# Last weight tap in two transfers, scratch loads a round sooner, and the last tile's inverse jobs a little later in a one-core FFT convolution

## The chip, the core and the metric

The kernel runs on one core of a Trainium2 chip. A core has a matrix engine (TensorE, PE in the profile, its weight loads PEld), a vector engine (DVE), a scalar engine (ACT), GpSimd (POOL) and SyncE (SP), which here issues nearly all DMA transfers, one after the other. ACT issues a few in the last tile. The metric is the time of one execution in microseconds on the device. Three executions of the kernel before took 270.08, 270.45 and 270.87 us; the median is 270.45 us.

## What is computed

The input `x` has 224 x 224 pixels of 96 channels, the weights `w` 7 x 7 taps of 96 x 96. The reference multiplies their two-dimensional transforms, which makes a circular convolution over the picture:

```python
wp = jnp.pad(w, ((0, H - K), (0, W - K), (0, 0), (0, 0)))
Xf = rfft2(x, axes=(1, 2))
Wf = rfft2(wp, axes=(0, 1))
Yf = jnp.einsum('bhwi,hwio->bhwo', Xf, Wf)
y  = irfft2(Yf, s=(H, W), axes=(1, 2)).astype(jnp.bfloat16)
```

## The kernel before

**Stages.** Along the height the kernel works with short transforms: 28 output rows need 34 input rows, and these become 17 slots (`NS`), most of them one complex frequency each. Along the width it convolves directly with the seven taps, split into even and odd pixels. Four stages follow from that.

- Weight preparation (`prep_jobs`). The raw weights lie in the tile `wq`, two rows for each of the 49 taps (a tap's input channels 0 to 47 and 48 to 95). A matmul of `wq` with a small matrix gives the transformed weights `WF` of a group of slots. Each of these matmuls reads columns from the whole length of `wq`, so the first of them needs every column of all 98 rows.
- Stage A (`a_jobs`, `f_jobs`): a matmul of 118 pixel rows with `Fm` gives the transformed pixels `xf`.
- Stage B (`b_round`): for one slot, DVE forms differences and sums `J` of `xf`; PE multiplies `xf` and `J` with `WF` (33 matmuls a round); ACT and DVE combine the sums in PSUM (tiles `tt_`, `u`, `v`), and POOL or DVE writes `yf`. Every three slots `yf` goes to a scratch tensor in DRAM (`scr`).
- Stage C (`c_jobs`): a tile's scratch comes back in another layout (`tt`, `tt2`), so that slots lie on partitions; a job is two matmuls with `Gm`, two evacuations, and now and then a store to `out`.

**Tiles.** The picture is cut into seven tiles of 32 columns. Tiles 0 and 1 run interleaved, tiles 2 to 6 one after the other, 17 rounds each. A round has two half rounds, and in the middle and at the end of a round `fills` lets other jobs in: `add(a, b, jobs)` spreads a list of jobs evenly over the half rounds from a to b. Stage A of the next tile and stage C of an earlier one are such lists. `CQ[t]` says how many jobs of tile t-2 and how many of tile t-1 run in tile t: in tile 5 four old and eleven new ones, in tile 6 (the last, `TL`) eleven new ones. The order of the instructions on every engine is the order of the program; there is no scheduler behind it.

**The scratch loads.** `queue_c(t - 1)` puts the five loads of tile t-1 (four `tt` and one `tt2`, the latter in four transfers) on a list, and `pump` issues from it as long as fewer than four `tt` buffers and one `tt2` buffer are taken. A finished unit of jobs frees its buffer and pumps again. In the kernel before, `queue_c` is called at round 3 of the tiles 2 to 6. SP waits in order, so a load that waits for the last scratch store of the tile before holds up what stands behind it.

**The start.** SP issues in this order: the halo pixels of both pixel groups (four transfers), the first tile's pixels of group 0 (two), ten weight transfers, then the pixels of group 1. The weights are cut into five chunks of columns; for each chunk the last tap's two rows go first and the 96 rows of the other taps second. The pixels of group 1 wait for the third chunk (`HOLD`). Every transfer counts on one of eight semaphores in turn, and waits for the transfer eight places before it. While the weights are under way PE runs dummy matmuls (`warm`): 17 at the start, and two times 11 between the first pixels' transforms and the weight preparation.

**The end.** In the last tile the scratch is in three parts. The first (slots 0 to 8, `scra`) is loaded back at round 11, the others (`scrb`) after the last round; then come 36 dummy matmuls, the second half of the inverse, and the last stores.

Of the kernel before, what the change touches and what calls it, by code (L numbers as in the profile page):

```python
# [17 lines left out]
NS = L // 2  # L18
# [29 lines left out]
HOLD = 2  # L48
# [8 lines left out]
def kernel(  # L57
# [7 lines left out]
    _, H, W, C = x.shape  # L65
    assert tuple(w.shape) == (KT, KT, C, C) and C == 96 and H == NJ * B and W % (2 * TW) == 0
    NT = W // (2 * TW)
    TL = NT - 1
    HB = JG * B
    R = HB + PAD  # L70
    PW = KT * KT
    FR = 2 * NS
    PW2 = 2 * PW
    C2 = C // 2
    assert NJ == 8
    SYNC = mybir.DependencyInfo(mybir.DependencyClass.Sync, mybir.DependencyReason.DATA)
# [57 lines left out]
    def dma(out_ap, in_ap):  # L134
        return DE.dma_start(out=out_ap, in_=in_ap)
# [18 lines left out]
    wqx = wtmp.tile([128, C - 1 + 127 * C + 1], BF16, name="wq")  # L154
    wq = wqx[0:PW2]
    WC = C * C - C2
# [18 lines left out]
    def load_x(t, jg):  # L175
        return load_rows(xbuf(t, jg), jg, t * 2 * TW, 2 * TW)

    wsrc = w.rearrange("kh kw i o -> (kh kw) (i o)")
# [2 lines left out]
    load_x(0, 0)  # L181
    wcut = [WC * c // NWC // 128 * 128 for c in range(NWC)] + [WC]
    wdma = []
    for c0, c1 in zip(wcut, wcut[1:]):
        for k, n in ((PW - 1, 1), (0, PW - 1)):
            wdma.append(dma(wqx[2 * k:2 * (k + n), c0:c1],
                bass.AP(wsrc.tensor, wsrc.offset + k * C * C + c0, [[C * C, n], [C2, 2], [1, c1 - c0]])))
    for d in load_x(0, 1):
        tc.add_manual_dep(d.ins, wdma[2 * HOLD + 1].ins.name, SYNC, reason="second pixels behind the weights")

    wu = cpool.tile([128, 128], BF16, name="wu")
    wur = wu[:].unsqueeze(1).to_broadcast([128, 4, 128])
# [2 lines left out]
    def warm(n):  # L195
        pwu = bank()
        for _ in range(n):
            TE.matmul(pwu[:].rearrange("p (a b) -> p a b", a=4), lhsT=wu[:, 0:128], rhs=wur, start=True, stop=True)
# [235 lines left out]
    def a_jobs(t):  # L434
        xf = new_xf(t)
        jobs = []
        for jg in range(2):
            for h in range(2):
                for (q, n) in ((0, 3), (3, 3), (6, 2)):
                    jobs.extend(a_bank(t, xf, xn_bufs[jg], h * PXC + 2 * q, n, jg, HALO + h * 8 + q))  # L440
            jobs.append(then_load(jobs.pop(), t + 1, jg))
        return jobs
# [23 lines left out]
    def jit(t, g):  # L466
        s0, s1 = JGB[g]
        n = s1 - s0
        xf = xf_tiles[t][0:C]
        xv = xf.rearrange("c p r s w j -> c p r s (w j)")  # L470
        b = jcount[0] % 3 if t < 2 else (jcount[0] - 2 * len(JGB)) % 2
        jcount[0] += 1
        Jb = J_bufs[b][0:C].rearrange("c (k s q) -> c k s q", k=7, s=3)
        for s in range(s0, s1):
            jbuf[(t, s)] = Jb[:, :, s - s0]

        def sub(o, a, b, op, cost):
            def f():
                load["v"] += 170 + cost / 1.92
                return VE.tensor_tensor(out=o, in0=a, in1=b, op=op)  # L480
            return f
        x0, x1 = xv[:, 0, :, s0:s1], xv[:, 1, :, s0:s1]
        c0, c1 = max(s0, REAL[0] + 1), min(s1, REAL[1])
        i0, i1 = c0 - s0, c1 - s0
        pd, rd, sd, qd = x1.ap
        dpl = bass.AP(x1.tensor, x1.offset - NJ, [pd, [NJ, 2], rd, sd, qd])
        return [
            sub(Jb[:, 0:4, 0:n].rearrange("c (k r) s q -> c k r s q", r=2), dpl,
                x0.unsqueeze(1).to_broadcast([C, 2, 2, n, PP]), ALU.subtract, 4 * PP * n),
            sub(Jb[:, 4, i0:i1], xv[:, 0, 0, c0:c1], xv[:, 0, 1, c0:c1], ALU.add, PP * (c1 - c0)),  # L490
            sub(Jb[:, 5:7, i0:i1], Jb[:, 0:4:2, i0:i1], Jb[:, 1:4:2, i0:i1], ALU.add, 2 * PP * (c1 - c0)),
        ]
# [152 lines left out]
    def c_jobs(t):  # L645
        jobs = []
        w0 = t * 2 * TW
        for gi, h in LT:
            hold = {}
            nq = 2 if gi < 2 else 3  # L650

            def mk_(q, gi=gi, h=h, nq=nq, hold=hold):
                def put(j0, nj, px, npx, row, col):
                    dma(out[0, j0 * B:(j0 + nj) * B, w0 + px:w0 + px + npx, :].rearrange("h w c -> h (w c)"),
                        hold["yo"][row:row + nj * B, col:col + npx * C])

                def f():
                    if q % 2 == 0:
                        hold["yo"] = new_yo()
                    tt = tt_tiles[(t, gi, h)]  # L660
                    yo = hold["yo"]
                    nj = 2 if q == 2 else 3
                    for b in range(2):
                        pb = bank()[0:nj * B, 0:4 * C]
                        TE.matmul(pb, lhsT=G[0:nj * FR, 0:nj * B],
                                  rhs=tt[0:nj * FR, 4 * q + 2 * b:4 * q + 2 * b + 2, :].rearrange("p w e -> p (w e)"), start=True, stop=True)
                        k = 2 * (q % 2) + b
                        evac(yo[0:nj * B, k * 4 * C:(k + 1) * 4 * C], pb, 4 * C)
                    if q == 1 and gi < 2:
                        put(gi * 3, 3, h * PXC, PXC, 0, 0)  # L670
                    elif q == 1:
                        put(6, 2, 0, 16, 0, 0)
                        for j in range(2):
                            put(6 + j, 1, 24, 8, 2 * B, j * 8 * C)
                    elif q == 2:
                        put(6, 2, 16, 8, 0, 0)
                    if q == nq - 1:
                        held[gi == 2] -= 1
                        pump()
                return f  # L680
            for q in range(nq):
                jobs.append(mk_(q))
        return jobs
# [11 lines left out]
    def queue_c(t):  # L695
        pend.extend((t, *k) for k in LT)
        pump()
# [6 lines left out]
    for p in range(3):  # L704
        for f in fj[p][0]:
            f()
    for n in (11, 11):
        warm(n)
    for f in prep_jobs(0):
        f()  # L710
# [22 lines left out]
    def fills(qs, k):  # L733
        def f():
            for q in qs:
                pace(q, k)
        return f
# [3 lines left out]
    def add(a, b, jobs):  # L741
        qs.append([a, b, jobs, len(jobs)])
# [15 lines left out]
    for r in range(NS + LAG):  # L758
# [32 lines left out]
        for t in range(2):  # L791
            s = r - LAG * t
# [15 lines left out]
    for t in range(2, NT):  # L808
        if t == TL:
            scr_tiles[t] = None  # L810
            scr_tiles[(t, 0)] = dr_pool.tile([TW, NJ, SA, 4 * C], BF16, name="scra")
            for i in range(2):
                scr_tiles[(t, 1 + i)] = dr_pool.tile([TW, NJ, (SB - SA, NS - SB)[i], 4 * C], BF16, name=f"scrb{i}")
        else:
            scr_tiles[t] = dr_pool.tile([TW, NJ, NS, 4 * C], BF16, name="scr")
        qs = []
        if t + 1 < NT:
            add(4 if t == 2 else 0, 26, a_jobs(t + 1))
        nold, nnew = CQ[t]
        k1 = 2 * NS if t < TL else 2 * NS - 9  # L820
        k0 = 10 if t in (2, TL) else 3
        km = k0 + -(-(k1 - k0) * nold // (nold + nnew))
        add(k0, km, cj[:nold])
        cn = c_jobs(t - 1)
        cj = cn[nnew:]
        add(km, k1, cn[:nnew])
        plan = {}
        for g, (s0, s1) in enumerate(JGB):
            if g + 1 < len(JGB) or t + 1 < NT:
                plan[s0 if g + 1 < len(JGB) else s0 - 1] = g  # L830
        for s in range(NS):
            now = ()
            if s in plan:
                g = plan[s]
                now = jit(t, g + 1) if g + 1 < len(JGB) else jit(t + 1, 0)
            if s == 3:
                queue_c(t - 1)
            if t in (3, 4):
                next(gp, None)
            if t == TL and s == SA + 2:  # L840
                sv = scr_tiles[(TL, 0)].rearrange("w j s (r e) -> (j s r) w e", r=2)
                for g in range(2):
                    for p0, p1 in ((0, 64), (64, KA)):
                        dma(tl_a[g][p0:p1], sv[g * KA + p0:g * KA + p1])
            b_round(t, s, fills(qs, 2 * s), fills(qs, 2 * s + 1), bool(now) or (t == TL and s >= NS - 3), now)
# [24 lines left out]
    for i, (g, q) in enumerate(order):  # L870
# [3 lines left out]
        k = i + 8 - LF  # L874
        if 8 <= k < len(order):
            live[order[k]] = first(*order[k])
        if q % 2 == 1:
            w0, c0 = TL * 2 * TW + (q - 1) * 4, (q % 4 - 1) * 4 * C
# [33 lines left out]
```

## Time and profile before

| | |
|---|---|
| profiled execution | 270.74 us, span on the core 269.0 us |
| granted TensorE clock, mean | 0.997 |
| PE busy | 257.9 us (96%), 5144 matmuls |
| DVE, ACT, POOL busy | 214.3, 195.5, 99.4 us |
| DMA | 46.78 MB, mean 174 GB/s |
| first matmul on the weights | 16.21 us |
| tile 5 begins, tile 6 begins | about 191 us, about 224 us |
| last matmul of stage B | 252.46 us |

All times inside the execution count from the start of its span. A busy PE in this table is not PE at its peak: matmuls are pipelined, and their ends are modelled. What decides is where PE waits. Idle time is listed with what ended it, for PE and for its weight loads (PEld) apart; the weight load stands ahead of its matmul and shows the longer idle time of the two. The helper that records every operation puts all of them on line 89, so groups are told apart by their tiles and not by lines.

### The profile page before, as it was taken

Reading aid. Unit: us, or ns where it says so; the run is one execution under the profiler, and the core shown is the slowest. Engines: PE = TensorE matmul, PEld = TensorE weight load, DVE = VectorE, ACT = ScalarE, POOL = GpSimd, SP = SyncE. Lnnn points to the kernel's source line nnn. Section 1 sums busy time; section 2 is a strip of 40 time slices with the busy share of each in tenths; the row PEclk is TensorE's granted clock in tenths of the full one; section 3 lists DMA queues with packets and bytes.
Section 4 is the critical chain, followed back from the end, with each engine's and each line's share of the span. In section 5 each row is a group of like instructions: output and inputs, shape, how many; then the busy total and the mean of one; then the engine's idle time right before and its main releaser. Section 6 shows DMA issues by size and latency. Waiting matters only on the chain.

```text
span 269.0 us, 12171 instructions
## 1 busy us (share of the span) xinstructions
PE 257.9 (96%) x5144; PEld 237.1 (88%) x5144; DVE 214.3 (80%) x457; ACT 195.5 (73%) x483; POOL 99.4 (37%) x156
## 2 busy tenths in 40 slices
PE   8899999999999999999999999999998999899993
PEld 3679999999998999999999998989997989779862
DVE  5649998889899788778787888777887889778724
ACT  5549988587974578988988789886986864467113
POOL 7782315363647435322322222234132242522100
PEclk9999999999999999999999999999999999999998
DMA  6948011811111597987976486989658834888866
GB/s 171 230 129 217 6 46 46 243 47 67 46 46 50 163 276 135 294 249 206 289 207 198 133 246 192 250 223 332 224 151 152 255 98 154 198 231 212 223 118 205
DMA packets 47014, 46.78 MB, mean 174 GB/s; under 512 B 35286, under 2 KB 37986, under 8 KB 46960
## 3 DMA queue, kind: packets, MB, share of 16 engines
q1 hardware_dynamic: 44672, 43.94, 59.2%
q10 hardware_dynamic: 2288, 2.06, 2.8%
q8 instruction: 40, 0.66, 1.1%
q14 instruction: 14, 0.11, 0.1%
HBM read 24.65 MB, written 21.33 MB: 171 GB/s over the span
## 4 chain that ended last, share of the span: by engine, by line
PE 64%; DMA 12%; DVE 11%; ACT 7%; issue 3%; SPq 2%; DVEq 0%; ACTq 0%
PE pb L89 64%; DMA tt<-scr 5%; DMA wq<-in_w_dram 5%; DVE J L89 4%; ACT WF L89 3%; ACT xf L89 2%; DVE v L89 2%; DVE WF L89 2%; SPq L89 2%; DMA xf<-scrb 2%; DVE u L89 1%; DMA scrb<-yf 1%; DVE yf L89 1%; DVE xf L89 0%; DVE tt L89 0%
## 5 line engine op out<-in xcount | busy, mean ns | idle before, releaser
L89 PE MATMUL pb<-WF,J 96*128 96x96 bf16 x2821 | 162.6, 206 | 1.1 <-DVE J L89 0.9
L89 PEld LDWEIGHTS <-J 96*128 96x128 bf16 x2821 | 138.0, 98 | 10.5 <-issue 2.2
L89 POOL TENSOR_TENSOR yf<-v,u 128x384 bf16<-128x384 f32 x79 | 81.4, 1042 | 147.3 <-issue 86.9
L89 ACT CAST xf<-pb 96x408 bf16<-96x408 f32 (+3 forms) x145 | 67.8, 490 | 8.9 <-PE pb L89 5.3
L89 PE MATMUL pb<-WF,xf 96*128 96x96 bf16 x952 | 59.9, 206 | 0.5 <-ACT xf L89 0.5
L89 DVE TENSOR_TENSOR J<-xf 96x1824 bf16<-96x1824 bf16 (+1 forms) x84 | 56.9, 716 | 0.1
L89 PEld LDWEIGHTS <-xf 96*128 96x128 bf16 x952 | 47.0, 98 | 0.7 <-ACT xf L89 0.6
L89 PE MATMUL pb<-Fm,xn 118*128 118x136 bf16 (+3 forms) x640 | 45.5, 199 | 0.2 <-DVE u L89 0.2
L89 PE MATMUL pb<-tt,Gm 102*84 102x384 bf16 (+1 forms) x132 | 32.7, 327 | 2.4 <-DMA tt<-scr 2.3
L89 ACT CAST WF<-pb 96x480 bf16<-96x480 f32 (+1 forms) x59 | 29.1, 577 | 5.3 <-PE pb L89 5.3
L89 PEld LDWEIGHTS <-xn 118*128 118x128 bf16 x640 | 30.3, 97 | 0.3 <-issue 0.3
L89 ACT CAST J<-pb 84x384 bf16<-84x384 f32 (+1 forms) x64 | 27.6, 488 | 2.3 <-PE pb L89 2.0
L89 ACT CAST yo<-pb 84x384 bf16<-84x384 f32 (+1 forms) x63 | 26.9, 482 | 2.7 <-PE pb L89 2.7
L89 DVE TENSOR_TENSOR J<-J 96x912 bf16<-96x912 bf16 (+2 forms) x42 | 24.2, 576 | 0.0
L89 PE MATMUL pb<-wq 98*128 98x120 bf16 (+1 forms) x288 | 21.3, 226 | 0.3 <-DMA wq<-in_w_dram 0.3
L89 PEld LDWEIGHTS <-wq 98*128 98x128 bf16 x288 | 19.5, 151 | 0.8 <-issue 0.8
L89 PE MATMUL pb<-wu 128*128 128x512 bf16 (+1 forms) x75 | 16.5, 382 | 1.1 <-DVE ct L89 1.1
L89 PEld LDWEIGHTS <-wu 128*128 128x128 bf16 (+1 forms) x75 | 8.8, 119 | 7.7 <-issue 2.4
L89 DVE TENSOR_TENSOR yf<-v,u 128x384 bf16<-128x384 f32 x26 | 14.9, 571 | 0.9
L89 PEld LDWEIGHTS <-Gm 102*84 102x84 bf16 (+1 forms) x132 | 11.0, 117 | 3.5 <-DMA tt<-scr 2.9
L89 ACT COPY xf<-xf 96x816 bf16<-96x816 bf16 (+3 forms) x20 | 11.3, 632 | 0.0
L89 DVE CAST WF<-pb 96x480 bf16<-96x480 f32 (+1 forms) x13 | 7.5, 611 | 4.7 <-PE pb L89 4.7
(386 smaller groups left out, 234.4 us busy)
## 6 DMA issues: line engine op xcount, KB each, us to landing
scr<-yf SPq DMA_DIRECT2D x30, 288.0 KB
xn<-in_x_dram SPq DMA_DIRECT2D x12, 672.0 KB
tt<-scr SPq DMA_DIRECT2D x24, 336.0 KB
out_dram<-yo SPq DMA_DIRECT2D x12, 252.0 KB
out_dram<-J SPq DMA_DIRECT2D x12, 252.0 KB
tt<-scr SPq DMA_DIRECT2D x6, 288.0 KB
WF<-in_x_dram SPq DMA_DIRECT2D x2, 672.0 KB
out_dram<-tt SPq DMA_DIRECT2D x8, 168.0 KB
```

The costliest lines, as they stand in the source:

```text
L89: r = fn(*a, **k)
```

## The change

Four things are done. First, the last tap's rows no longer go with every chunk: after the second chunk of the other taps come two transfers, and each takes eight of sixteen pieces of 573 columns from both rows, alternating (pieces 0, 2, 4, ... and pieces 1, 3, 5, ...). There are seven weight transfers in place of ten; the pixels of group 1 still wait for the third chunk. Second, the dummy matmuls ahead of the weight preparation are 20 in place of 22. Third, in tiles 3, 4 and 5 `queue_c` is called at round 2. Fourth, the eleven stage C jobs of the last tile spread over half rounds 12 to 26 and not 10 to 25.

```diff
-    for c0, c1 in zip(wcut, wcut[1:]):
-        for k, n in ((PW - 1, 1), (0, PW - 1)):
-            wdma.append(dma(wqx[2 * k:2 * (k + n), c0:c1],
-                bass.AP(wsrc.tensor, wsrc.offset + k * C * C + c0, [[C * C, n], [C2, 2], [1, c1 - c0]])))
+    LR = PW - 1
+    wp = WC // 16
+    for c, (c0, c1) in enumerate(zip(wcut, wcut[1:])):
+        wdma.append(dma(wqx[0:2 * LR, c0:c1],
+                        bass.AP(wsrc.tensor, wsrc.offset + c0, [[C * C, LR], [C2, 2], [1, c1 - c0]])))
+        if c == 1:
+            for z in range(2):
+                dma(wqx[2 * LR:PW2, 0:WC].rearrange("p (a z b) -> p a z b", z=2, b=wp)[:, :, z],
+                    bass.AP(wsrc.tensor, wsrc.offset + LR * C * C + z * wp, [[C2, 2], [2 * wp, 8], [1, wp]]))
     for d in load_x(0, 1):
-        tc.add_manual_dep(d.ins, wdma[2 * HOLD + 1].ins.name, SYNC, reason="second pixels behind the weights")
+        tc.add_manual_dep(d.ins, wdma[HOLD].ins.name, SYNC, reason="second pixels behind the weights")
...
-    for n in (11, 11):
+    for n in (10, 10):
         warm(n)
...
-        k1 = 2 * NS if t < TL else 2 * NS - 9
-        k0 = 10 if t in (2, TL) else 3
+        k1 = 2 * NS if t < TL else 2 * NS - 8
+        k0 = {2: 10, TL: 12}.get(t, 3)
...
-            if s == 3:
+            if s == (3 if t in (2, TL) else 2):
                 queue_c(t - 1)
```

In the compiled order of the instructions the change shows in these places only. On PE two dummy matmuls are gone, and the stage C matmuls of tile 6 stand later. On SP the weight transfers are as told; in tile 3 one scratch load stands ahead of a scratch store, in tile 4 two loads stand ahead of a small copy for `GB` and a scratch store, in tile 5 six load transfers stand ahead of an output store and a seventh ahead of a scratch store; in tile 6 the four transfers that load `scra` stand ahead of an output store. On ACT the evacuations of tile 6's stage C jobs stand later among the rounds. DVE and POOL have the same order as before. The second transfer of the last tap waits, by its semaphore, until the first has landed completely: their pieces alternate in the same two rows, and the program treats that as an overlap. The three later chunks stand behind that wait in SP's order.

## The prediction

> **What bounds the kernel.** The page comes first. PE is busy nearly everywhere; the early slices and the tail are the exception, and the chain of waits spends most of its share on PE and the next largest on DMA.
>
> ```profile
> span 269.0 us, 12171 instructions
> PE 257.9 (96%) x5144; PEld 237.1 (88%) x5144; DVE 214.3 (80%) x457; ACT 195.5 (73%) x483; POOL 99.4 (37%) x156
> ...
> PE 64%; DMA 12%; DVE 11%; ACT 7%; issue 3%; SPq 2%; DVEq 0%; ACTq 0%
> ```
>
> The chain in order of time tells where that DMA share lies. Columns: start, length, what.
>
> ```profile
> 3.40 6.14 DMA wq<-in_w_dram
> 9.55 6.52 DMA wq<-in_w_dram
> 16.07 0.14 issue
> 16.21 0.69 PE pb L89 x8
> ...
> 198.20 5.54 DMA tt<-scr
> 203.74 0.04 issue
> 203.79 26.07 PE pb L89 x527
> ...
> 231.54 7.14 DMA tt<-scr
> ```
>
> The first chunk of the weights was issued at 3.40 and landed at 9.54; that released the semaphore for the fifth chunk, issued at 9.55, landed at 16.07. From there ACT and DVE, then PE carry the chain without a break, so a later landing delays everything. The two `tt` pieces are scratch loads of tiles 5 and 6.
>
> The waits of the weight loads, and three rows of PE's timeline, give their size.
>
> ```profile
> PEld L89 <- DMA tt<-scr: 2.9, 4, 1.2
> ```
>
> ```profile
> 203.79 0.52 PE L89 MATMUL pb<-tt,Gm 102*84 102x384 bf16 x2 [1.10 <-DMA tt<-scr]
> ...
> 232.21 0.52 PE L89 MATMUL pb<-tt,Gm 102*84 102x384 bf16 x2 [0.96 <-DMA tt<-scr]
> ...
> 238.73 0.52 PE L89 MATMUL pb<-tt,Gm 102*84 102x384 bf16 x2 [0.28 <-DMA tt<-scr]
> ```
>
> PE lost 2.9 us to scratch loads: about 1.25 in tile 5 (the weight load's own figure is 1.2), the other 1.7 in tile 6. Tiles 3 and 4 have no such wait. SP's timeline says why tile 5's load was late.
>
> ```profile
> 192.31 0.35 SPq L89 DMA_DIRECT2D scr<-yf  x1
> 196.91 0.32 SPq L89 DMA_DIRECT2D out_dram<-J  x1
> 197.76 0.35 SPq L89 DMA_DIRECT2D scr<-yf  x1
> 198.20 7.90 SPq L89 DMA_DIRECT2D tt<-scr  x7
> ```
>
> Tile 4's last store went out at 192.31, but the loads stood behind an output store and a scratch store of tile 5 that were not ready until 197.
>
> Last, sums by stretch: length, busy of PE, PEld, DVE, ACT, POOL, granted clock, DMA share, GB/s.
>
> ```profile
> 1.00:7.60 6.60, 5.89 (x22) 2.41 (x22) 3.63 (x24) 3.96 (x5) 5.41 (x27) 1.00 0.80 205
> 1.00:9.20 8.20, 7.41 (x61) 3.79 (x62) 5.19 (x26) 4.94 (x7) 6.83 (x35) 1.00 0.85 209
> 1.00:14.00 13.00, 12.21 (x140) 6.85 (x141) 8.11 (x31) 7.09 (x12) 10.35 (x52) 1.00 0.92 214
> ...
> 20.60:21.10 0.50, 0.34 (x8) 0.35 (x9) 0.50 (x1) 0.31 (x2) 0.26 (x1) 1.00 0.00 0
> 21.10:21.30 0.20, 0.20 (x7) 0.20 (x5) 0.10 (x2) 0.16 (x1) 0.00 (x0) 1.00 1.94 276
> ```
>
> By 7.6 us 6.6 x 205 = 1.35 MB had moved, which is all pixels before the weights (1.00 MB) and the first chunk (0.34), whose landing was told at 9.54: a lag of 1.9 us. By 14.0 it was 2.78 MB, everything to the fifth chunk, told at 16.07: 2.0 us.
>
> **The weights: +1.9 us.** The second tap transfer waits for the first to land, and chunks three to five stand behind it on SP. The first half tap stands behind two chunks in the queue, 1.70 MB in all (1.00 + 2 x 0.344 + 0.018). By the row to 9.20 that has moved by 9.2 us; with the lag of 1.95 it lands at 11.15. By then everything issued has landed and the queues are empty. SP issues the second half (0.25 to 0.44 us in the weight transfers' rows; 0.35) and at 11.5 the third chunk. An issue into empty queues brings first bytes 0.95 us later: the next tile's pixels were issued at 20.24 (SP's timeline), and the stretch to 21.10 shows no byte. So bytes flow from 12.45. Chunks three to five are 1.07 MB, with the half tap 1.09; at 214 to 237 GB/s (the latter is the stretch from 11 to 12) they take 4.6 to 5.1, until 17.25. The lag lies between 0 and 2.0; the 2.0 hold the uneven finish of sixteen engines after ten transfers, and here they start level after a drain, so I take 0.75: 18.0, against 16.07. Ends for the range: with the best stretch of the start (301 GB/s, from 4 to 5) and no lag 16.1, so +0; with 214 and the full lag 19.5, so +3.4.
>
> At this place the Trainium skill speaks against the change (DMA: Bandwidth & Descriptors, "Why a DMA increments its semaphore by 16 and not by 1"): a transfer runs on the largest number of engines, up to 16, that divides the slowest dimension of both patterns. By that, two rows of eight pieces stay on two engines, as the tap's two rows did. On sixteen engines a half tap would take 1.1 KB at 14.5 KB/us each, 0.1 us; on two 0.6. No row here tells engines apart. By the rule the first half lands 0.5 later and the forecast would be 270.3.
>
> Three issues fewer on SP are worth nothing, since SP then stands waiting. The two dummy matmuls (4.91 us for 22, so 0.45) end in a wait for weights either way: nothing. The pixels of group 1 wait for the third chunk, with the same lag landed at about 14.7; they move 0.72 MB behind the fifth chunk, some 3 us at 237, until 20.3 and a lag. Their matmuls began 2.99 us after the first on weights (16.21 to 19.20), so are wanted at 21.1: hidden, barely; without that cover up to 0.5.
>
> **Tiles 3 to 5: -1.25 us.** Tile 5: the loads follow the store of 192.31 directly. A store and the load behind it are 2.4 us apart at the end (253.89 to 256.30), so the first load goes out at about 195 and, with its old 5.54, lands at 200.5; PE wants it at 202.5. The wait goes. What is late next: seven loads take SP 7.9 us, so the output store that was ready at 196.9 leaves at about 202, and round 2's scratch store at about 203.5 and not 197.76. The `yf` buffer of that store is wanted four groups later, at round 12, some 20 us on; the output buffer four units later. Both are hidden; without the cover, 5 us on POOL. Bounds: 0 to -1.25. Tile 3: a scratch store passes behind one load and its wait, about 2 us later; tile 4: a `GB` copy and a store behind two loads. PE waits for neither, so nothing.
>
> **Last tile: -1.35 us.** The first job goes from the middle of round 5 to that of round 6. PE's rows there give 1.40 us a round without jobs and 0.33 a job, so it is wanted at 232.6, after the landing at 232.2. The fifth job (first of `tt2`) is wanted at 237.4, after 237.1, the sixth at 238.5, where its load lands at 238.7: 0.2 us of wait are left. DVE needs J for round 6, ready at 232.55 (1.93 + 0.62), and PE asks at about 232.2: another 0.2 of new wait. So 1.7 - 0.4 = 1.3; and `u` of round 12, which waited 1.02 us for ACT and PE, comes ahead of one job more, so 1.35. Bounds: -1.75 (all waits, no new one) to 0 (see below).
>
> **The sum** is +1.9 - 1.25 - 1.35 = -0.7 on 270.74 for the profiled execution, whose span is 269.0 with 1.74 around it. It lies 0.29 above the median; -0.7 on 270.45 gives 269.8.
>
> **Rivals.** (1) The clock falls. Dummy matmuls end at 15.4 (10.98 + 20 x 0.223), so PE idles 2.65 us until 18.05. In the stretch from 266 to 269 the granted clock is 0.74, which is half speed from 267.4 on, 2.7 us after the last matmul ended (264.75). If it falls, the 48 matmuls of the first preparation, 3.15 us, take up to twice that; ACT and DVE evacuate beside them, so I take 1.5 of the 3.15: 271.3, slower. It decides from a landing of 18.1 on. Against it: a gap of 2.65 is just under. The Trainium skill (TensorE: Matmul & The Clock Gate, "What's actually happening") has the clock fall after an idle window of about 3.4 us that runs free, by which it stays up at 2.65; the trace, with 2.7, sets the shorter limit.
>
> (2) The tail takes back the last tile's gain. One output store (252 KB, 1.1 us at 237) now goes behind the `scra` loads, nearer to the stores and loads that end the kernel, where the DMA share is over 1. For it: the last `scrb` pieces wait on landings. Against it: the share falls to 0.31 from 254 to 256. If the whole 1.1 is lost: 270.9.
>
> (3) The first half tap holds nothing up, the weights land as before or sooner: -2.6, 267.9. For it: taps need fewer issues. Against it: the wait stands in the compiled order, and nothing can overtake two chunks in the queue by the lags above.
>
> **The numbers.** Chances: the sum 0.45 (269.0 to 270.3), weights later than 18.3 without a clock change 0.15 (270.3 to 272.0), rival 1 0.20, rival 2 0.11, rival 3 0.09. A difference of 0.3% (0.81 us) is about what a measurement can tell from none. Faster needs 269.64 or less: 0.27 of the sum's 0.45 and rival 3 give 0.36. Slower needs 271.26: half of the late weights, 0.7 of rival 1 and a quarter of rival 2 give 0.25. Same has 0.39. The range runs from 268.4 to 271.8; rivals 1 and 2 lie inside, rival 3 and the worst of the late weights outside.
>
> **What will show it.** Right: a gap of some 5 us on SP between the two tap transfers; a stretch near 11 to 12.4 without DMA; the first matmul on `wq` at about 18; no `tt` wait in tile 5 and 0.2 in tile 6; loads of tile 5 issued near 195. Wrong: the first matmul on `wq` before 16.5 (first step), a `tt` wait still at tile 5's sixth round (second), PE idle over 0.5 in rounds 5 to 9 of tile 6 or the last `scrb` piece no earlier after the last `yf` (third). A granted clock under 1 near 18 is rival 1.

## The result: slower by 1.45%

| | before | after |
|---|---|---|
| median of six executions, us | 270.54 (270.08 to 270.87) | 274.13 (273.68 to 275.70) |
| profiled execution, us; its span | 270.74; 269.0 | 273.68; 271.9 |
| granted TensorE clock, mean, in the six executions | 0.997 in the profiled one | 0.981 to 0.993 |
| first matmul on the weights | 16.21 | 18.91 |
| first matmul of stage B | 20.76 | 24.32 |

The ratio is 1.0145, with a 95% interval of 1.0121 to 1.017. The forecast was 269.8 us with a range to 271.8: the change is slower, and by more than the range held.

The page of the profiled execution, its first lines and the chain's shares by engine:

```profile
span 271.9 us, 12166 instructions
PE 259.0 (95%) x5142; PEld 238.0 (88%) x5142; DVE 214.1 (79%) x457; ACT 194.7 (72%) x483; POOL 98.5 (36%) x156
...
PE 64%; DMA 12%; DVE 11%; ACT 7%; issue 3%; SPq 2%; ACTq 0%; DVEq 0%
```

These shares are those of before almost to the point, so they do not tell where the 2.9 us between the two spans went. The chain in order of time does (start, length, what):

```profile
4.48 6.47 DMA wq<-in_w_dram
10.95 0.02 issue
10.97 0.25 SPq L89
...
12.52 6.03 DMA wq<-in_w_dram
18.56 0.35 issue
```

The transfer issued at 4.48 is the first half of the last tap, landed at 10.95. The second half went out at 10.97, and the last chunk of the weights at 12.52; in the kernel before, the last chunk went out at 9.55. It landed at 18.56 and not at 16.07: 2.49 us later. What the queues and the clock did meanwhile is in the sums by stretch (length, busy of PE, PEld, DVE, ACT, POOL, granted clock, DMA share, GB/s):

```profile
9.00:10.00 1.00, 1.00 (x40) 0.98 (x37) 1.00 (x3) 1.00 (x4) 0.68 (x3) 1.00 0.21 54
10.00:11.00 1.00, 0.95 (x35) 0.87 (x33) 1.00 (x2) 0.63 (x2) 0.73 (x4) 1.00 0.11 25
11.00:12.00 1.00, 1.00 (x11) 0.46 (x8) 1.00 (x3) 0.58 (x1) 0.75 (x5) 1.00 0.04 7
12.00:13.00 1.00, 1.00 (x7) 0.47 (x5) 0.12 (x1) 0.00 (x0) 0.74 (x4) 1.00 0.53 76
13.00:14.00 1.00, 1.00 (x7) 0.41 (x6) 0.00 (x0) 0.00 (x0) 0.72 (x5) 1.00 0.79 274
...
19.00:20.00 1.00, 1.00 (x14) 1.00 (x15) 0.57 (x1) 0.26 (x1) 0.84 (x3) 0.58 0.59 184
20.00:22.00 2.00, 2.00 (x27) 2.00 (x25) 1.71 (x3) 1.47 (x4) 0.77 (x2) 0.50 0.00 0
22.00:23.00 1.00, 1.00 (x22) 1.00 (x21) 0.59 (x2) 0.88 (x3) 0.00 (x0) 0.72 0.00 0
```

From 9 to 13 us the DMA engines are nearly idle (54, 25, 7, 76 GB/s), the drain that the wait makes. And the clock is at half speed from about 19.2 (0.58 of the stretch from 19) to 22.6 (0.72 of the one from 22). PE's timeline shows both effects in one row. The kernel before has this one:

```profile
16.21 3.15 PE L89 MATMUL pb<-wq 98*128 98x100 bf16 x48 [0.32 <-DMA wq<-in_w_dram]
```

The changed kernel has, with two rows from later tiles:

```profile
18.91 4.01 PE L89 MATMUL pb<-wq 98*128 98x100 bf16 x48 [3.45 <-DMA wq<-in_w_dram]
...
217.44 0.76 PE L89 MATMUL pb<-WF,J 96*128 96x96 bf16 x14 [0.38 <-DVE u L89]
...
239.32 0.70 PE L89 MATMUL pb<-tt,Gm 102*84 102x384 bf16 x2 [0.30 <-ACT J L89]
```

The matmuls start 2.70 us later, after 3.45 us in which PE stood still, and the 48 take 4.01 us and not 3.15, which is 0.86 more. Together that is the 3.56 us by which stage B starts later. The two lower rows are waits that before did not have, on DVE in tile 5 and on ACT in tile 6; the three waits for `tt` that stood there before are gone. Stage B's delay against before, taken at the same matmul of stage B in both traces, runs like this:

| where | delay of after, us |
|---|---|
| stage B starts | 3.56 |
| tile 5 begins | 3.71 |
| past the old `tt` wait of tile 5 | 2.42 |
| end of tile 5 | 2.96 |
| tile 6, past the old wait at 232.2 | 1.54 |
| tile 6, past the row at 239.32 | 2.60 |
| tile 6, past the old wait at 238.73 | 1.80 |
| end of stage B | 2.63 |

So the gains hoped for in tile 5 (1.29) and in tile 6 (1.42) are made, and 0.54 and 1.06 of them are given back within a few rounds; the third old wait brings another 0.80, of which nothing is left at the end. In tile 6 a part of each step is only order: a stage C job that now stands later (0.33 us by the prediction's rows) counts first as a gain and then as a loss.

SP's timeline of tile 5 shows the loads right behind the store of 196.02, as the change says:

```profile
196.02 0.35 SPq L89 DMA_DIRECT2D scr<-yf  x1
199.46 4.67 SPq L89 DMA_DIRECT2D tt<-scr  x6
204.25 2.04 SPq L89 DMA_DIRECT2D out_dram<-J  x1
```

### The profile page after: what moved, and what is told of

Its sections match the earlier page's. It is cut to its first block, busy times and chain, and to the rows that moved or that the text cites. A ratio compares the mean times of both kernels' runs of the same rounds, so it can differ in the third digit from the quotient of the medians.

```text
span 271.9 us, 12166 instructions
## 1 busy us (share of the span) xinstructions
PE 259.0 (95%) x5142; PEld 238.0 (88%) x5142; DVE 214.1 (79%) x457; ACT 194.7 (72%) x483; POOL 98.5 (36%) x156
## 4 chain that ended last, share of the span: by engine, by line
PE 64%; DMA 12%; DVE 11%; ACT 7%; issue 3%; SPq 2%; ACTq 0%; DVEq 0%
PE pb L89 64%; DMA wq<-in_w_dram 5%; DVE J L89 5%; ACT xf L89 3%; SPq L89 2%; ACT WF L89 2%; DMA xf<-scra 2%; DMA tt<-scr 2%; DVE WF L89 2%; DVE v L89 2%; DMA xf<-scrb 1%; DMA scrb<-yf 1%; DVE u L89 1%; DVE yf L89 1%; ACT J L89 1%
## 5 line engine op out<-in xcount | busy, mean ns | idle before, releaser
L89 PE MATMUL pb<-wq 98*128 98x120 bf16 (+1 forms) x288 | 22.1, 234 | 3.5 <-DMA wq<-in_w_dram 3.5
L89 PEld LDWEIGHTS <-wq 98*128 98x128 bf16 x288 | 20.3, 151 | 3.9 <-issue 3.9
```

The lines of the kernel that those rows point to most:

```text
L89: r = fn(*a, **k)
```

## The experiments

Two theories stood at first. One: the second half of the tap waits for the first because their pieces alternate, so both lie within the same stretch of the same two rows, and the drained queue and the clock that falls behind it are the whole loss; the other two edits gain. The rival: the last tap's small pieces, or the later edits, are themselves slow. Four kernels ran beside the kernel before, which had a median of 270.13 us there (268.94 to 271.08).

**No wait between the halves.** The change as it is, with the two halves told to be disjoint, which they are.

```diff
-            for z in range(2):
-                dma(wqx[2 * LR:PW2, 0:WC]...[:, :, z], ...)
+            dz = [dma(wqx[2 * LR:PW2, 0:WC]...[:, :, z], ...) for z in range(2)]
+            tc.declare_no_dep(dz[1].ins, dz[0].ins, reason="disjoint pieces of two rows")
```

> The changed kernel, but the two tap transfers are declared independent (their pieces are disjoint), so the second is issued without waiting for the first to land; pieces, places and everything else as in the changed kernel. Theory (the hold on SP costs 2.5 us of landing, and the idle PE behind it costs the clock another 1.0 us): the first matmul on wq goes from 18.9 back to 15.5 to 16.3, the granted clock stays at 1.00 up to tile 6, and the time falls by 3.5 to 4 us, to 269.5 to 270.2. Rival (the short pieces, or the tap behind two chunks, are what is slow): the first matmul stays beyond 17.5 and the time beyond 272.5. A second rival (the later tiles cost the time, not the start): 273 to 274, whatever the start does.

Measured: 269.99 us (269.59 to 270.82), 0.9993 of before (0.9976 to 1.001). SP's timeline has all seven weight transfers in one run of 5.6 us, where after has 10.02, and PE's wait is short:

```profile
3.10 5.60 SPq L89 DMA_DIRECT2D wq<-in_w_dram  x7
13.65 1.18 SPq L89 DMA_DIRECT2D WF<-in_x_dram  x2
```

```profile
15.90 3.14 PE L89 MATMUL pb<-wq 98*128 98x100 bf16 x48 [0.45 <-DMA wq<-in_w_dram]
```

The mean granted clock of that execution is 1.000. Taking the wait away takes away all of the loss, 4.1 us. It does not leave the 2.6 us gain that the third rival of the prediction had for this case.

**The start alone.** The weights and the dummy matmuls as changed; the loads and the last tile's jobs as before.

```diff
-        k1 = 2 * NS if t < TL else 2 * NS - 8
-        k0 = {2: 10, TL: 12}.get(t, 3)
+        k1 = 2 * NS if t < TL else 2 * NS - 9
+        k0 = 10 if t in (2, TL) else 3
...
-            if s == (3 if t in (2, TL) else 2):
+            if s == 3:
```

> Only the first and second edit (tap in two transfers, 20 dummy matmuls); scratch loads and last tile as before. Theory: the whole loss is here, +3.6 us with one clock drop and up to +5 with more, and none of the gain of the later tiles: 274.1 to 275.8, that is 0 to 1 above the changed kernel. Rival (the moved loads and jobs cost the time): 270 to 271.

Measured: 274.44 us (273.98 to 275.63), 1.0162 of before (1.0131 to 1.0192). The start alone costs 4.3 us, more than the whole change. PE's row and two stretches of this run tell when the clock fell:

```profile
19.04 4.19 PE L89 MATMUL pb<-wq 98*128 98x100 bf16 x48 [3.58 <-DMA wq<-in_w_dram]
```

```profile
17.00:18.00 1.00, 0.00 (x0) 0.00 (x0) 0.00 (x0) 0.00 (x0) 0.88 (x2) 1.00 0.93 223
18.00:19.00 1.00, 0.00 (x0) 0.00 (x0) 0.00 (x0) 0.00 (x0) 0.82 (x4) 0.57 1.00 276
```

A mean of 0.57 in the stretch from 18 is half speed from 18.14 on. The last dummy matmul had ended at 15.46, so the clock fell 2.7 us into the gap, while PE still stood.

**The rest alone.** The reverse: weights and dummy matmuls as before, the other two edits as changed.

> Only the third and fourth edit (scratch loads at round 2 in tiles 3 to 5, last tile's jobs in half rounds 12 to 26); weights and dummy matmuls as before. Theory (from comparing the two traces matmul by matmul: tile 5 gains 1.3 and gives 0.5 back, the last tile gains 0.3, the tail gives 0.2 back): -0.7 us, 269.6 to 270.1. The recorded prediction's sum for these two edits: -2.6, 267.9. Rival (moved loads cost): above 270.9.

Measured: 269.48 us (268.91 to 270.36), 0.998 of before (0.996 to 1.0001). The two later edits are worth 0.65 us by the medians, near the limit of what can be told from nothing, and a quarter of the 2.6 that the prediction added up.

**The clock kept up.** The change with 33 dummy matmuls ahead of the weights and not 20, so that PE does not stand still while the weights are late.

```diff
-    for n in (10, 10):
+    for n in (11, 22):
         warm(n)
```

> The changed kernel with 33 dummy matmuls in place of 20 ahead of the weight preparation, so PE is busy until about 18.4 and the weights still land at 18.6. Theory (the clock falls because PE idles 3.4 us): the granted clock stays 1.00, the 48 matmuls on wq take 3.1 us again and not 4.0, and the time is 0.9 to 1.5 us under the changed kernel, 272.6 to 273.2, with less spread between executions. Rival (idle time does not matter, the late landing is the whole of it): 273.7 to 274.5 as the changed kernel.

Measured: 272.49 us (271.98 to 273.07), 1.0089 of before (1.0058 to 1.0119). PE's timeline and two stretches of the same kernel:

```profile
12.80 5.99 PE L89 MATMUL pb<-wu 128*128 128x512 bf16 x27
18.63 3.11 PE L89 MATMUL pb<-wq 98*128 98x100 bf16 x48
```

```profile
18.00:20.00 2.00, 2.00 (x27) 1.68 (x26) 0.94 (x2) 0.69 (x2) 1.66 (x6) 1.00 0.63 178
20.00:22.00 2.00, 2.00 (x44) 2.00 (x43) 1.84 (x5) 2.00 (x5) 0.79 (x2) 1.00 0.04 12
```

The first matmul on the weights is late here too, at 18.63, but the clock holds at 1.00 and the 48 matmuls take 3.11 us. This parts the loss of the start: the lateness is worth about 2.5 us (272.49 against 269.99 without the wait; a few tenths of it may be the dummy matmuls' own, since the fifth chunk's last landing count in this trace is at 17.98 and PE began 0.65 later, against 0.35 in after), the clock some 1.6 (274.13 against 272.49, two groups of runs on different chips, whose medians of before differ by 0.4; by the ratios, 0.0056 of 270, 1.5).

What was left open was why the later edits bring a quarter of what was reckoned. The next four ran beside before at 270.15 us (269.04 to 272.39).

**The last tile alone.**

```diff
-        k1 = 2 * NS if t < TL else 2 * NS - 9
-        k0 = 10 if t in (2, TL) else 3
+        k1 = 2 * NS if t < TL else 2 * NS - 8
+        k0 = {2: 10, TL: 12}.get(t, 3)
```

> Only the last tile's inverse jobs are moved (half rounds 12 to 26); weights, dummy matmuls and tiles 2 to 5 are as before. Theory A (the prediction's step): 1.7 us of waits for scratch loads go in tile 6, 0.4 comes back, so stage B ends about 1.3 us earlier and the time falls by about 1.35, to 0.995 of before. Theory B (ACT's order): the loads' waits go as said, but ACT's evacuations of the second and third job now stand behind a store of the first scratch part that ACT issues itself and that waits for POOL's yf, so PE meets a new wait of about 1 us near the tenth half round after; stage B ends only 0.3 to 0.5 earlier, and the stores and loads that end the kernel, which get an output store close ahead of them, take about as much back: 0.999 to 1.001 of before.

Measured: 270.11 us (269.33 to 270.86), 0.9996 of before (0.9978 to 1.0014): no difference. Within the trace, tile 6 gains 1.41 us against before past the old wait, loses 1.07 at the next jobs (the order of the jobs included), and 0.32 remain at the end of stage B.

**The last tile, with the scratch store of slots 3 to 5 on SP.** In the last tile ACT issues the stores of the first scratch part itself. ACT's timeline in after shows what that does once the jobs are later:

```profile
236.35 0.41 ACT L89 ACTIVATE tt__6990<-pb 128x288 f32<-128x288 f32 x1 [1.65 <-DVE v L89]
238.35 0.33 ACTq L89 DMA_DIRECT2D scra<-yf  x1
238.80 1.61 ACT L89 CAST J<-pb 84x384 bf16<-84x384 f32 x4 [2.04 <-PE pb L89]
```

The four casts evacuate the first two jobs. They stand behind a store that waits for POOL's `yf` (two of these, 1.96 us from 236.36, so until 238.3), and ACT is idle from 236.8 to 238.3. In before the order was the reverse: casts at 232.60, store at 235.39.

```diff
-                puts.append(lambda: put(SE))
+                puts.append(lambda: put(DE if s == 5 else SE))
```

> The last tile's jobs are moved as in the change, and the store of the first scratch part's slots 3 to 5 is issued by SP and no longer by ACT; nothing else is changed. Theory B (ACT's order): the new PE waits near 239 to 240 us, 1.1 us together, are gone, since ACT's evacuations no longer stand behind that store; stage B ends 1.0 to 1.6 earlier than before, and the time is 0.995 to 0.998 of before, 0.5 to 1.0 us under the run with ACT's store. Rival C (the wait is the bank's or POOL's own, whichever engine issues the store): the waits near 239 to 240 stay, and the time is that of the run with ACT's store, within 0.3 us. A price that could hide the gain: SP now waits for POOL's yf ahead of its loads and output stores.

ACT's timeline of this run has the casts right behind the activation:

```profile
233.14 0.41 ACT L89 ACTIVATE tt__6995<-pb 128x288 f32<-128x288 f32 x1 [1.66 <-DVE v L89]
233.44 1.60 ACT L89 CAST J<-pb 84x384 bf16<-84x384 f32 x4
```

PE's new wait on ACT is gone (of the new waits in this tile only 0.23 us on DVE's `J` at 231.81 stays), and tile 6 gains 1.31 us by the end of stage B where the run before this one gained 0.32. So ACT's order is shown as the cause of the wait at 239, and its price is 1.0 us. The time did not follow: 270.47 us (269.54 to 272.74), 1.0024 of before (0.9995 to 1.0052). Five of the twelve executions took over 270.8. The profiled one, at 269.96, shows 17.5 us from the last matmul of stage B to the end of the span where before has 16.7; what the long ones lost was not recorded. The expectation held for the wait and failed for the time.

**Tiles 3 to 5 alone.**

```diff
-            if s == 3:
+            if s == (3 if t in (2, TL) else 2):
                 queue_c(t - 1)
```

> Only the scratch loads of tiles 3, 4 and 5 are queued a round sooner. Theory A (the prediction's step): tile 5's wait of 1.25 us goes and nothing takes its place; stage B ends 1.2 earlier, time about 0.9955 of before. Theory B (DVE is next): 1.2 is gained at round 6 of tile 5, and about 0.55 is given back by the end of that tile, where PE waits for DVE's sums; stage B ends about 0.7 earlier, time 0.997 to 0.998 of before.

Measured: 269.86 us (269.07 to 270.90), 0.9998 of before (0.9979 to 1.0017). In the trace 1.30 us are gained at the old wait and 0.53 given back at the row that PE has in after as well:

```profile
213.55 0.76 PE L89 MATMUL pb<-WF,J 96*128 96x96 bf16 x14 [0.37 <-DVE u L89]
```

That is the size of theory B's give-back, but not a delay that DVE would have caused in any case. In before, the same matmuls began at 214.49, ahead of the DVE instruction that this run's row waits for:

```profile
214.49 0.76 PE L89 MATMUL pb<-WF,J 96*128 96x96 bf16 x14
```

```profile
214.62 0.35 DVE L89 SCALAR_TENSOR_TENSOR u<-pb,tt__6369 128x192 f32<-128x192 f32 x1
```

In this run that instruction comes first:

```profile
213.15 0.35 DVE L89 SCALAR_TENSOR_TENSOR u<-pb,tt__6369 128x192 f32<-128x192 f32 x1
```

By the semaphores in the trace's records, the first of these matmuls waits for ACT in the four kernels that load tile 5's scratch as before, and for DVE in all nine that load it sooner. So the wait is new in the program. That the matmul gets another buffer in PSUM, one that DVE has to empty, would fit; it was not tried.

The net 0.77 is still more than the time shows, and runs in which tile 5 is untouched say why. The rows at the old wait, from the run with the last tile alone and from the one with SP's store:

```profile
202.78 0.52 PE L89 MATMUL pb<-tt,Gm 102*84 102x384 bf16 x2 [0.24 <-DMA tt<-scr]
```

```profile
203.52 0.52 PE L89 MATMUL pb<-tt,Gm 102*84 102x384 bf16 x2 [0.62 <-DMA tt<-scr]
```

The same code, with the loads issued at 198.05 and 198.42 (198.20 in before), waited 0.24 and 0.62 us, where the profile of before has 1.10; the run of the start alone has 0.49. The wait that the prediction took away whole was the longest of four.

**Everything, without the two faults.** The change with the halves told to be disjoint and SP's store.

> The whole change, with the two halves of the last tap declared disjoint (no wait between them) and the store of slots 3 to 5 issued by SP. If the two causes found are the ones that cost (the wait between the halves, and ACT's store ahead of the evacuations): stage B ends 1.8 to 2.6 us earlier than before, and the time is 0.992 to 0.996 of before, the fastest of all kernels here. If the end of the kernel takes back what stage B gains (its stores and loads have a length of their own behind the last output stores): 0.996 to 0.999.

Measured: 269.65 us (268.56 to 271.94), 0.9997 of before (0.9973 to 1.002). Stage B ends 2.0 us earlier in the trace, but the span is only 1.1 shorter: the end takes back 0.9. That is the second case of the expectation in kind, though the ratio lies just above its 0.996 to 0.999 and cannot be told from 1.

**The last output store behind the last scratch store.** In the run before this one the last scratch store goes out at 251.66, an output store of 252 KB at 251.12, and the load behind the scratch store leaves only at 256.34; before has 2.41 us between store and load. So two kernels let that output store pass behind: one on top of the last, one with the later edits alone. They ran beside before at 270.46 us (269.11 to 271.52).

```diff
+                    if q == 1 and t == TL - 1 and (gi, h) == LT[-1]:
+                        lateput.append(lambda: put(gi * 3, 3, h * PXC, PXC, 0, 0))
-                    if q == 1 and gi < 2:
+                    elif q == 1 and gi < 2:
...
+    lateput.pop()()
     tail[0] = 2
```

> As the run with the whole change, no wait between the halves and SP's store, and in addition the last output store of tile 5's jobs (252 KB), which there left SP 0.54 us ahead of the last scratch store, leaves right behind it. Theory T (the tail's price is that output store, ahead of the last scratch stores in the queues): the last scratch piece lands and is loaded again 2.4 to 3.2 us after its store is issued, not 4.7; the end comes 0.7 to 1.5 us sooner, time 268.2 to 269.1 with before at 270.15, 0.993 to 0.996 of it. Rival U (the bytes have to move anyway, and only change places): the loads of the last scratch pieces, issued meanwhile, take longer by what the store gains, and the time stays within 0.3 us of the run without this edit (269.65), 0.998 to 1.0.

> The scratch loads a round sooner and the last tile's jobs moved as in the change, weights and dummy matmuls as before, ACT still issuing the store of slots 3 to 5; the last output store leaves SP right behind the last scratch store. Theory T: the store of the last scratch piece to its load takes 2.4 to 3.2 us and not 4.0, and the time falls by 0.5 to 1.0 against the run without this edit (269.48), to 268.5 to 269.0. Rival U: 269.2 to 269.8.

Measured: 269.50 us (268.99 to 271.06), 0.9972 of before (0.9953 to 0.9992), and 269.65 us (269.14 to 270.67), 0.9979 (0.9958 to 1.0). The chain at the end, first of the run with everything and the output store ahead, and of the same with it behind:

```profile
251.66 4.66 DMA scrb<-yf
...
256.34 2.98 DMA xf<-scrb
```

```profile
252.64 4.11 DMA scrb<-yf
...
256.77 4.01 DMA xf<-scrb
```

Then of the run with the later edits alone, and of the same with the output store behind:

```profile
252.69 4.01 DMA scrb<-yf
...
256.72 2.97 DMA xf<-scrb
```

```profile
252.25 2.99 DMA scrb<-yf
...
255.26 4.57 DMA xf<-scrb
```

Store and load together took 7.6 and then 8.1 us, and 7.0 and then 7.6; before, 6.4. With the output store behind, nothing is won: the store's time fell from 4.7 to 4.1 and from 4.0 to 3.0, and the load's rose from 3.0 to 4.0 and to 4.6. So the theory that this one store's place sets the end falls; the rival, that the same bytes have to move and only change places, fits the four chains, but with one profile of each (that of the first of these kernels is its slowest execution, 271.06 us) it is not shown. The first of these two kernels is the only one whose whole interval lies below 1; by its medians it is 0.96 us under before, 0.35%.

**One row of the tap in each transfer.** The last run returns to the weights: the halves cut by rows, so that neither a wait nor a declaration is needed. Before stood at 270.22 us.

```diff
-                dma(wqx[2 * LR:PW2, 0:WC].rearrange("p (a z b) -> p a z b", z=2, b=wp)[:, :, z],
-                    bass.AP(wsrc.tensor, wsrc.offset + LR * C * C + z * wp, [[C2, 2], [2 * wp, 8], [1, wp]]))
+                dma(wqx[2 * LR + z:2 * LR + z + 1, 0:WC].rearrange("p (a b) -> p a b", b=wp),
+                    bass.AP(wsrc.tensor, wsrc.offset + LR * C * C + z * C2, [[C2, 1], [wp, 16], [1, wp]]))
```

> The whole change, but the two transfers of the last tap take one row each (sixteen pieces of 573 columns) and not alternate pieces of both rows, so the two share no row of the tile and none waits for the other. Theory A (the wait between the halves is all of the weights' loss): weights issued without a break by about 8.2, first matmul on them at 15.6 to 16.5, clock at full speed, time 0.997 to 1.001 of before, as where the halves were declared disjoint. Rival R (the alternating pieces cost in themselves, by the engines that they land on): with one row of sixteen pieces a transfer spreads over more engines, and the first matmul on the weights comes 0.3 to 0.6 sooner than the 15.90 of that run, at 15.3 to 15.6.

Measured: 270.25 us (269.55 to 271.09), 1.0006 of before (0.9987 to 1.0025).

```profile
15.90 3.15 PE L89 MATMUL pb<-wq 98*128 98x100 bf16 x48 [0.45 <-DMA wq<-in_w_dram]
```

First matmul on the weights at 15.90, exactly as with the alternating pieces and no wait. In the trace each of these transfers is a single piece of 18,336 bytes with one landing count, where a half of alternating pieces has two. So the rival's transfer over more engines was not made, and whether that would bring the weights sooner stays open; one count in place of two did not bring them later. The wait was all of the loss.

## Why the prediction was wrong

**The weights: right in kind, short by 0.6 us.** The drain was foreseen, and its steps stand beside the trace like this: first half landed 11.15, measured 10.95; third chunk issued 11.5, measured 11.26; first bytes of that chunk 12.45, measured about 12.7 (76 GB/s in the stretch from 12, at 274 in full, is 0.28 us; its first packet in the trace began at 12.62). The bytes of the last 1.09 MB: 0.87 had moved by 16 (76 + 274 + 274 + 250 GB/s of four stretches), the rest takes 0.9 us at 238, so counted in bytes they ended near 16.9, where the prediction had 17.25. The step that failed is the lag: between 0 and 2.0 it took 0.75, because sixteen engines would start level after a drain. Measured, 18.56 - 16.9 is 1.65, close to the 1.9 and 2.0 us of the rows that it had itself read. So the landing came at +2.49 and not +1.9.

The trace's own records show why the reason given for 0.75 fails. They have sixteen landing counts for the fifth chunk, and these came from 17.17 to 18.56, 1.39 us apart; in before, from 13.87 to 16.07, 2.20 apart. After the drain the engines finished a little closer together, but far from level. The chunk's last packet (its packets are the only ones of 3,744 bytes) ended at 17.48, and in before at 15.11, so 1.08 and 0.96 us lie between it and the landing. The rest of the 1.65 and 2.0 is a matter of counting: the sum of bytes books as the chunk's what engines further ahead had already moved of the next transfer. The prediction's lags of 1.9 and 2.0 therefore held two things; the drain left the time behind the last packet as it was and only shortened the uneven finish, from 1.0 to 0.6 us.

**Rival 1, the clock, with a chance of 0.20, is what happened.** It was to decide from a landing of 18.1 on; the landing was 18.56, and PE stood still for 3.45 us, not 2.65. So the misjudged lag made this case likelier. The price, 1.5 us, came out at 0.86 in the profiled execution and about 1.6 in the median. Each of the six executions shows it: means of 0.981 to 0.993 over some 272 us are 3.8 to 10 us at half speed, of which up to 2 may lie at the end of the kernel, since the 23 executions of before that ran beside the first four experiments had means of 0.996 to 1.000.

The limit of 2.7 us that the prediction read from one trace was one draw, too. In the start alone the clock fell 2.7 us into the gap; in the run with the later edits alone it fell 1.8 us after the last matmul of the kernel, which ended at 263.99 (0.95 in the stretch from 264 to 266 is half speed from 265.8); in the run with the tap by rows it was still full 4.4 us after the last one (263.90; 1.00 in the stretch from 265 to 268.3). So a gap of 2.65 us was not safe: it lies within this spread. The rule of the Trainium skill weighed there (TensorE: Matmul & The Clock Gate, "What's actually happening") has the clock fall after an idle window of about 3.4 us that runs free. The trace does not agree that PE must stand still for so long, by the 1.8 and 2.7 us; a window that runs free fits the spread.

**Two dummy matmuls fewer: "nothing" is not shown.** They end at 15.46 and not at 15.9, and with the weights late those 0.45 us are part of the gap of 3.45. Whether 22 would have kept the clock up was not tried; 33 did.

**The tap on two engines.** By the rule of the Trainium skill (DMA: Bandwidth & Descriptors, "Why a DMA increments its semaphore by 16 and not by 1") two rows of eight pieces stay on two engines. The trace agrees: the first half has two landing counts, at 10.92 and 10.95, so engines can be told apart after all. Of the price put on two engines little appeared: the half was to land at 11.65 and the time to be 270.3; its packets took the 0.5 us from 9.41 to 9.92, but half of that while the second chunk's were still moving (until 9.66), and it landed at 10.95.

**Tiles 3 to 5: -1.25 us reckoned, 1.29 gained in the trace, 0.3 in the medians, which is not told from nothing.** Where the wait was and what takes it away was right. Two things were not: "what is late next" looked along SP's queue alone, and a new wait of PE for DVE, which the kernels with the old order of loads do not have, takes back 0.54; and the 1.10 us were one draw of a landing that varies, 0.24, 0.49 and 0.62 in three other executions of the same code.

**Last tile: -1.35 us reckoned, 0.32 gained.** The waits for loads went as said. The step that failed is the new wait: 0.2 us was given to DVE's `J`, and that wait came (0.22 us at 235.02), while ACT's own queue, with the store that waits for POOL, was not read, and cost 1.0. Rival 2 is partly right too: in the run with the later edits alone the end of the kernel took back 0.5 us (1.0 earlier at the end of stage B, 0.5 at the end of the span).

**The sum.** Start +4.3, later edits -0.65: +3.66, against a measured 3.59. The forecast had +1.9 and -2.6.

## What to carry to other kernels

When a change cuts one transfer into interleaved pieces, look first whether the pieces' rows overlap as the framework sees them: here the wait between two disjoint halves emptied the queues and cost 4 us, and a cut by rows cost nothing. An engine that stands still has two prices, the lateness and the clock behind it, and a gap worked out just under a limit that one trace shows should be given nearly even chances. Before a wait is booked as gain, read every queue that is then first in line, the issuing engine's own included (a store on ACT holds up ACT's evacuations), and take a DMA wait from one profile as one draw.

## What was not expected of the hardware

- The clock fell between 1.8 and more than 4.4 us after PE's last matmul, and in one gap after 2.7. Once down it stayed at half speed for 3.4 us in the profile of after (19.2 to 22.6, with PE busy throughout) and for 6.8 in that of the start alone (18.1 to 25.0, with PE standing still for the first 0.9), and by the mean clocks for 8 to 10 us in other executions.
- After a drain, the sixteen landing counts of one chunk still came 1.39 us apart, against 2.20 in the full stream of the kernel before, and the last came 1.08 us after the chunk's last packet, against 0.96.
- The landing of the same scratch loads, issued at the same place within 0.4 us, took 5.6, 4.7 and 5.1 us to the end of the wait in three executions, a spread larger than the net gain under study.
